# Spectral mixing plus a product-key expert layer on one core: another order of folds and transposes at the front, key products a block later, and table checks that begin one block earlier

## The chip, the cores and the metric

The kernel runs on one core of one Trainium2 chip. The metric is the device time of one launch in microseconds, the median of three runs. Lower is better.

## The reference

The output is the sum of three things for x of 2048 x 512 floats. With xn the layer norm of x over its 512 columns,

```
out = x + A(xn) + B(xn)
A:  a = xn @ Wd_re.T;  b = xn @ Wd_im.T;  y = Ws_re @ a - Ws_im @ b     (real part of a 2-D Fourier transform)
B:  q = xn @ w_q                    (32 heads, 2 x 128 each)
    s1, s2 = q1 @ k1.T, q2 @ k2.T   (64 keys each)
    the best 2 of s1 and of s2 give 4 candidates, the best 2 of them the experts and, by softmax, their weights g
    out += sum over heads and experts of g * gelu(xn . u[e]) * v[e]     (4096 experts)
```

The tables Ws and Wd come in as inputs. The kernel uses that they are Fourier tables, and it checks this on the chip.

## The kernel before

**Front (lines 230 to 560).** x stands in four groups g of 4 x 128 rows, taken in the order G = (1, 0, 2, 3). For each group VectorE and ScalarE normalize it (ln). fold(k, g) (line 358) uses the symmetry of the Fourier tables: sums (k = 0) or differences (k = 1) of quarter rows give a tile q, in six or seven VectorE instructions, whose first is fold_t (353) and whose last two write q (363 and 364). fold_row(k) (366) does the same for one single row. main(k, g) (374) multiplies q with a table on TensorE (385) and adds up over the four groups in PSUM; evict copies the result out (428). In this part there also stand the following. m_mul(0, ..) (145) makes the key products m of stage 0 (keys times a slice of w_q, so that scores come straight from x); m_scale and m_parts (line 217) scale and split them. xpose(i) (439) transposes one of the 16 tiles of x: four transposes on TensorE (445), the high 16-bit half by ScalarE (448), the low half either by a product with a negated identity idn and ScalarE (450 and 452) or by VectorE alone (454). sides() (398) makes border columns by 16 VectorE multiply-adds (394 and 396), to which GpSimd adds two rows (415 and 416).

**Scores.** Eight stages j of 16 tiles i follow: TensorE makes the scores of tile i (820), ScalarE copies them (825), VectorE takes maxima and indices (828 and 832). m_stage makes the key products of the next stage from w_q in seven steps: a load of w_q on SP (131), copies by ScalarE (155 and 160), a difference by GpSimd (163) or VectorE (157), and products on TensorE (141). The table MST (for stage 0 MST0) says behind which tile each step goes. From stage 1 on, x's halves go to a scratch tensor; in the order of SP, the first 14 of these stores stand ahead of the first loads of w_q.

**Blocks.** Then come 14 blocks b of 128 tokens. u_part(b, cg) multiplies the block with 512 experts' u (980, tile z) and ScalarE applies the gelu (983). g_mm(b, tg) builds weights g from one-hot tiles L and R that VectorE makes (1004, 1012, 1015) and TensorE multiplies (1017). w_part(b, tg) multiplies weights and gelus: VectorE (1028, tile g), ScalarE (1033) and VectorE again (1036). v_part multiplies with v (1045). z tiles take turns in a few PSUM banks; in block 1, tile 7 takes the bank of tile 4. z of blocks 0 and 1 comes first, with w_part(0, ..) and g_mm(0, ..) between; then each block's v_part is done while the next one's g and w and the z of the one after it are made. The last two token blocks are done by gathering rows: GpSimd fetches rows of u and v (1071), VectorE takes dot products with the normalized x (1087, tile px; px itself is made at 269 from xs, loaded at 1080), ScalarE and GpSimd sum up (1100, 1105).

Ahead of the first v_part, the rows of these two blocks that part A made are taken from one scratch tensor to another: a load of oy from y_d (1321), an adding transfer of x from GpSimd (1322), a store to o_d (1323), twice.

**Checks.** paced(k, mm) (1280) takes two lists of work one piece a step. One holds the fits: the largest magnitude of a piece of w_q, u or v (1215, 1216, 1222). The other holds the compares: a tile cx of a Fourier table is loaded on SP (755 and 756) and compared with its mirrored parts on VectorE (763 to 797), and ScalarE sums the magnitudes (802 and 804). VectorE's work comes two steps of its list behind the load, ScalarE's two behind that. `later` and `hold` bind a step to the product mm it follows.

The order on each engine is set by a scheduler from the order of the code, from the dependences it sees, and from added ones (pace, follow, hold); the loads wait in SP's queue one behind another.

Of the kernel before, what the change touches and what calls it, by code (L numbers as in the profile page):

```python
# [8 lines left out]
F32 = mybir.dt.float32  # L9
# [27 lines left out]
def tile_fnet_peer(ctx, tc, x, ca, cb, c5, wt, wf, wr, wq, kt, ut, vn, uv, out):  # L37
# [146 lines left out]
    def m_scale(j, pm, at=None):  # L184

        if at is not None:
            nc.vector.tensor_copy(at, one)
        mp = MP[j % 2]
        w = 1 if at is None else 3
        mx = mp.tile([P, KD + w], F32, tag="mx" if w == 1 else "mx3", name=f"mx{j}")  # L190
        m = mp.tile([P, 2, KD, 512], F16, tag="m", name=f"m{j}")
        for kd in range(KD):
            nc.scalar.activation(m[:, 0, kd, :], pm[kd], AF.Abs, scale=1.0 if at is None else at,
                                 accum_out=mx[:, kd:kd + 1])
        if w == 3:
# [6 lines left out]
        sc = mp.tile([P, 2], F32, tag="msc", name=f"msc{j}")  # L202
        nc.vector.tensor_scalar(sc[:, 0:1], q[:, 0:1], 2.0 ** 13, None, op0=ALU.mult)
        nc.vector.tensor_scalar(sc[:, 1:2], p[:, 0:1], 2.0 ** -14 / XS, None, op0=ALU.mult)
        if w == 3:
            nc.vector.tensor_scalar(wsc[:, 0:2], q[:, 1:3], 2.0 ** 12, None, op0=ALU.mult)
            nc.vector.scalar_tensor_tensor(wsc[:, 4:5], p[:, 1:2], 2.0 ** -26, p[:, 2:3], op0=ALU.mult, op1=ALU.mult)
            nc.vector.scalar_tensor_tensor(smx, q[:, 0:1], 2.0 ** 11, wsc[:, 4:5], op0=ALU.mult, op1=ALU.mult)
            nc.vector.tensor_scalar(inv1, p[:, 0:1], 2.0 ** -12 / XS, None, op0=ALU.mult)
        M[j] = m, sc[:, 1:2]  # L210
        MS[j, "s"] = sc[:, 0:1]

    def m_parts(j, pm):
        m, sc = M[j][0], MS[j, "s"]
        for kd in range(KD):
# [69 lines left out]

    FF = {}
    SM = {}

    x5 = da.tile([1, 2, 512], F32, name="x5")
    nc.scalar.dma_start(x5, x[2:4, 0, 0:1].rearrange("q p d -> p q d"))  # L290
# [2 lines left out]
    def ln(g, n):  # L293

        for q in range(4):
            if n == 0:
                st = da.tile([P, 6], F32, tag="st", name=f"st{g}_{q}", bufs=2)
            else:
                st = (FF[0, G[0]][:, 0] if n == 1 else SM[n - 1])[:, 6 * (q % 2):6 * (q % 2) + 6]
            nc.vector.bn_stats(st, xn[g][:, q])  # L300
            nc.vector.bn_aggr(mvs[:, g, q, :], st)
        var = mvs[:, g, :, 1]
        SM[n] = da.tile([P, 12], F32, tag="sm", name=f"sm{g}", bufs=2)
        sm = SM[n].rearrange("p (a q) -> p a q", a=3)
        nc.scalar.activation(sm[:, 0], var, AF.Sqrt, bias=eps)
        nc.vector.reciprocal(sm[:, 1], sm[:, 0])
        nc.vector.scalar_tensor_tensor(sm[:, 0], var, 1e-5, sm[:, 1], op0=ALU.add, op1=ALU.mult)
        nc.vector.scalar_tensor_tensor(sm[:, 2], sm[:, 0], -0.5, sm[:, 1], op0=ALU.mult, op1=ALU.mult)
        nc.vector.scalar_tensor_tensor(rstd[:, g], sm[:, 2], 1.5, sm[:, 1], op0=ALU.add, op1=ALU.mult)
        end = nc.vector.scalar_tensor_tensor(negm[:, g], mvs[:, g, :, 0], -1.0, rstd[:, g], op0=ALU.mult, op1=ALU.mult)  # L310
        if g == 0:
            nc.vector.tensor_scalar(nm0[:, 0], negm[:, 0, 2:4], not0, None, op0=ALU.mult)
            nc.vector.tensor_scalar(nm0[:, 1], rstd[:, 0, 2:4], not0, None, op0=ALU.mult)
        for q in (0, 2, 1, 3):
            t = xn[g][:, q]
            b, r = negm[:, g, q:q + 1], rstd[:, g, q:q + 1]
            if g == 0 and q > 1:
                b, r = nm0[:, 0, q - 2:q - 1], nm0[:, 1, q - 2:q - 1]
            if n == 0 and q % 2 == 0:
                norm(t, t, 4 * q + g)  # L320
            else:
                nc.scalar.activation(t, t, AF.Identity, bias=b, scale=r)
        if g == 0:
            for q in range(2):
                nc.scalar.activation(x5[:, q], x5[:, q], AF.Identity, bias=negm[0:1, 0, q + 2:q + 3],
                                     scale=rstd[0:1, 0, q + 2:q + 3])
        return end

    def fold_d(k, t, f, o, after=None):
# [19 lines left out]
    def fold_t(k, g):  # L349
# [3 lines left out]
        nc.vector.tensor_tensor(t, xn[g][:, 0:2], xn[g][:, 2:4], op=op)  # L353

    def fold(k, g, after=None):

        if after is None:
            fold_t(k, g)
# [4 lines left out]
        nc.vector.tensor_tensor(Q[k][g][:, 0, c], o[:, 0, c], o[:, 1, c], op=ALU.add)  # L363
        FF["end"] = nc.vector.tensor_tensor(Q[k][g][:, 1, c], o[:, 0, c], o[:, 1, c], op=ALU.subtract)

    def fold_row(k):
# [3 lines left out]
        if k:  # L370
            pace(i, FF["end"])
        fold_d(k, r[:, :, 0:512], r[:, :, 512:], Q[1][0][0:1, 0:1] if k else s5.unsqueeze(1))

    PP = {}
# [23 lines left out]
    def sides():  # L398


        f = FF["t"][:, 0, 0:4]
        nc.vector.tensor_copy(f[:, 0:2], Q[0][G[0]][:, :, 256])
        nc.vector.tensor_copy(f[:, 2:4], c5s[:, :, G[0]])
# [32 lines left out]
    idn = da.tile([P, P], F16, name="idn")  # L436
    nc.gpsimd.tensor_scalar(idn, ident, -1.0 / XS, None, op0=ALU.mult)

    def xpose(i, sub=False):

        p = (pb if sub and i // 4 % 2 else pc)(f"xp{i}")
        src = xn[i % 4][:, i // 4]
        for kd in range(KD):
            c = slice(kd * P, (kd + 1) * P)
            nc.tensor.matmul(p[:, c], src[:, c], ident, start=kd == 0, stop=kd == KD - 1 and not sub,
                             is_transpose=True, skip_group_check=True)
        pv = p.rearrange("p (k n) -> p k n", k=KD)
        nc.scalar.activation(xt[i][:, 0], pv, AF.Copy, scale=XS)
        if sub:
            nc.tensor.matmul(p, idn, xt[i][:, 0].rearrange("p k n -> p (k n)"), start=False, stop=True,  # L450
                             skip_group_check=True)
            nc.scalar.activation(xt[i][:, 1], pv, AF.Copy, scale=XS)
# [36 lines left out]
    wrs = uf[13][0:1, 0:129]  # L489
    nc.sync.dma_start(wrs, wr)  # L490

    for t in range(2):
        m_mul(0, t, (0, 1))
    for n, g in enumerate(G):
# [14 lines left out]
        if n == 0:  # L509
            for t in range(2):  # L510
                m_mul(0, t, (2, 3))
            for t in range(2, 4):
                m_mul(0, t, range(KD))
    evict(0)
    m_scale(0, MS[0, "p"], FF[0, G[-1]][:, 0, 0:1])
    m_parts(0, MS[0, "p"])
    nc.scalar.activation(k16[:, 0], K[0], AF.Copy, scale=sk)
    nc.vector.scalar_tensor_tensor(k16[:, 1], K[0], sk, k16[:, 0], op0=ALU.mult, op1=ALU.subtract)
    for n, g in enumerate(G):
        if n:  # L520
            fold(1, g)
        if g == 0:
            fold_row(1)
# [53 lines left out]
    def part_b(safe, stS, stP, stE, xt, u_sb, cmp_p):  # L577
# [953 lines left out]
```

## Time and profile before

| | before |
|---|---|
| median of 3 runs | 1092.44 us |
| the runs | 1088.45, 1094.63, 1092.44 us |
| profiled execution, its own time | 1090.09 us |
| its span | 1088.3 us |
| mean granted clock of TensorE | 0.995 |
| TensorE busy | 1060.8 us (97%) |
| VectorE, ScalarE, GpSimd busy | 959.6, 716.3, 608.8 us |
| DMA | 196.78 MB, mean 181 GB/s |

In a timeline, a row gives start and length in us, the engine, the line, the operation, out<-in, the count of instructions taken together, and in square brackets the idle time ahead with what ended it. SPq is the queue from which SyncE issues DMAs; its rows give the time of issue, not the landing.

### The profile page before, as it was taken

What the parts mean: (1) busy time and instruction counts of PE and PEld (TensorE: products, weight loads), DVE (VectorE), ACT (ScalarE), POOL (GpSimd) and SP (SyncE); (2) the same over time, 40 slices, a digit from 0 to 9 for tenths busy, and PEclk for the clock granted to TensorE, in tenths of its full rate; (3) what the DMA queues carried; (4) which work ended last, traced back from release to release, by engine and by line L of the source; (5) the groups of instructions that cost most, each with busy time, mean ns of one, the idle gap of its engine ahead of it and who ended that gap; (6) DMA issues with size and microseconds to landing.
All of it is one profiled execution on the core that took longest, in us unless ns stands there. A gap on an engine that the chain in (4) does not pass through costs nothing. (4 is left out here: it accounts for less than half of the span.)

```text
span 1088.3 us, 28489 instructions
## 1 busy us (share of the span) xinstructions
PE 1060.8 (97%) x11070; PEld 693.4 (64%) x11070; DVE 959.6 (88%) x2748; ACT 716.3 (66%) x1326; POOL 608.8 (56%) x553
## 2 busy tenths in 40 slices
PE   5899999999999999999999999999999999999997
PEld 4354555454544544896876958769587785867853
DVE  7978797979999999989999998999999987999871
ACT  3566657679797857545767667676666766767641
POOL 0013547588787955225655566565568766556622
PEclk9899999999999999999999999999999999999999
DMA  8257152536445341278766766775678667675611
GB/s 332 86 204 261 52 197 94 175 125 219 167 136 197 104 157 66 73 250 240 230 179 202 213 203 222 223 223 183 194 214 276 201 193 231 216 232 186 192 31 52
DMA packets 84936, 196.78 MB, mean 181 GB/s; under 512 B 10770, under 2 KB 27559, under 8 KB 84792
## 3 DMA queue, kind: packets, MB, share of 16 engines
q1 hardware_dynamic: 63898, 123.55, 33.8%
q0 software_dynamic: 20736, 71.31, 22.1%
q8 instruction: 88, 1.44, 0.5%
q14 instruction: 56, 0.46, 0.1%
q10 hardware_dynamic: 158, 0.01, 0.0%
HBM read 177.74 MB, written 17.10 MB: 179 GB/s over the span
## 5 line engine op out<-in xcount | busy, mean ns | idle before, releaser
L820 PE MATMUL s<-m,xq 128*128 128x512 f16 x1536 | 338.9, 379 | 0.0
L980 PE MATMUL z<-xb,u 128*128 128x128 f16 x5376 | 306.8, 219 | 1.2 <-DVE y L1060 1.2
L980 PEld LDWEIGHTS <-u 128*128 128x128 f16 x5376 | 301.5, 98 | 4.2 <-issue 1.3
L1045 PE MATMUL v<-v,act 128*128 128x512 f16 x1344 | 298.3, 379 | 0.0
L1105 POOL TENSOR_TENSOR ov<-ov,ga 128x512 f32<-128x512 f32 x128 | 183.8, 1436 | 186.4 <-ACT ga L1100 145.9
L820 PEld LDWEIGHTS <-xq 128*128 128x128 f16 x1536 | 148.3, 98 | 171.4 <-issue 0.2
L1045 PEld LDWEIGHTS <-act 128*128 128x128 f16 x1344 | 128.4, 98 | 146.5
L1071 POOL DMA_INDIRECT ga<-in_uv_dram,eix x128 | 159.3, 1245 | 46.0 <-POOL ov L1105 34.9
L1004 DVE TENSOR_TENSOR L<-io_lam,cmp 128x2048 f16<-128x2048 f16 x112 | 154.8, 1397 | 15.1 <-PE g L1017 15.0
L828 DVE MAX8 vals<-ss 128x8 f32<-128x64 f32 x1024 | 152.6, 216 | 17.1 <-ACT ss L825 17.0
L983 ACT ACTIVATE act<-z,scl 128x512 f32<-128x512 f32 x112 | 76.0, 682 | 103.1 <-PE z L980 102.6
L832 DVE FIND_INDEX8 idx<-vals,ss 128x8 uint16<-128x256 f32 x256 | 107.2, 419 | 0.0
L825 ACT ACTIVATE ss<-s,wsc 128x512 f32<-128x512 f32 x112 | 75.5, 681 | 43.1 <-PE s L820 33.8
L1100 ACT ACTIVATE ga<-ga,za 128x512 f32<-128x512 f32 x128 | 92.3, 722 | 9.4
L1033 ACT ACTIVATE act<-g 128x1024 f16<-128x1024 f32 x56 | 73.2, 1309 | 22.0 <-DVE g L1028 19.9
L1087 DVE SCALAR_TENSOR_TENSOR ga<-ga,px 128x512 f32<-128x512 f32 x128 | 85.8, 678 | 0.1
L1036 DVE TENSOR_TENSOR act<-g,act 128x1024 f16<-128x1024 f32 x56 | 72.9, 1303 | 14.5 <-ACT act L1033 14.3
L802 ACT ACTIVATE cx<-cx 128x896 f32<-128x896 f32 x64 | 60.6, 946 | 37.5 <-DVE cx L782 21.6
L1028 DVE SCALAR_TENSOR_TENSOR g<-act,scl,g 128x1024 f32<-128x1024 f32 x56 | 71.5, 1280 | 5.1 <-ACT act L983 3.1
L163 POOL TENSOR_TENSOR wq<-wq,wh 128x1024 f16<-128x1024 f32 x26 | 55.5, 2135 | 24.3 <-DMA cx<-in_ca_dram 15.9
L1017 PEld LDWEIGHTS <-L 128*128 128x128 f16 x1792 | 51.8, 96 | 8.4 <-DVE L L1004 1.6
L776 DVE TENSOR_TENSOR cx<-cx 128x512 f32<-128x512 f32 (+2 forms) x61 | 47.1, 804 | 11.1 <-DMA cx<-in_cb_dram 11.0
(281 smaller groups left out, 1298.8 us busy)
## 6 DMA issues: line engine op xcount, KB each, us to landing
cx<-in_cb_dram SPq DMA_DIRECT2D x50, 448.0 KB
wq<-in_wq_dram SPq DMA_DIRECT2D x32, 512.0 KB
fit<-in_wq_dram SPq DMA_DIRECT2D x28, 512.0 KB
uv<-in_ut_dram SPq DMA_DIRECT2D x16, 512.0 KB
uv<-in_vn_dram SPq DMA_DIRECT2D x16, 512.0 KB
cx<-in_cb_dram SPq DMA_DIRECT2D x28, 224.0 KB
xq<-in_x_dram SPq DMA_DIRECT2D x8, 512.0 KB
xt_d<-xq SPq DMA_DIRECT2D x16, 256.0 KB
```

Of the source, the lines that this page charges most:

```text
L820: mm = nc.tensor.matmul(ps, xt[i][:, l, kd, :], m[:, r, kd, :], start=(n == 0), stop=(n == 3 * KD - 1))
L825: done = nc.scalar.activation(s.rearrange("p g e -> p (g e)"), ps, AF.Copy, scale=inv)
L828: nc.vector.max(vals[:, i, w, :, h], s[:, g, :])
L832: nc.vector.max_index(idx[:, i, w].rearrange("p k h -> p (k h)"), vals[:, i, w, 0:2].rearrange("p k h -> p (k h)"), s[:, w * HC:g + 1, :]. ...
L980: mm = nc.tensor.matmul(p[:, cc * P:(cc + 1) * P], ug[:, l, c % 2, kd, :], xb[:, r, kd, :], start=(n == 0), stop=(n == 3 * KD - 1))
L983: GL[mm.ins.name] = nc.scalar.activation(act[:, cg * 4:cg * 4 + 4, :].rearrange("p c n -> p (c n)"), p, AF.Gelu_apprx_tanh, scale=zsc)
L1004: nc.vector.tensor_tensor(L.rearrange("p t (l two) -> p t l two", two=2), io_lam.rearrange("p (l two) -> p l two", two=2).unsqueeze(1).to_ ...
L1045: mm = nc.tensor.matmul(pv, w16[:, c, :, l], vg[:, r, c % 2, :], start=(c == 0 and k == 0), stop=(c == NC - 1 and k == 2))
L1071: nc.gpsimd.indirect_dma_start(out=t, out_offset=None, in_=uv, in_offset=bass.IndirectOffsetOnAxis(ap=eix[:, n].rearrange("p k h -> p (k h ...
L1087: nc.vector.scalar_tensor_tensor(t, t, 1.0, T["x"], op0=ALU.mult, op1=ALU.mult, accum_out=T["z", n][:, s:s + 1])
L1100: nc.scalar.activation(t, t, AF.Copy, scale=z)
L1105: T["a"] = nc.gpsimd.tensor_tensor(o, o, t, op=ALU.add)
```

## The change

Front:

- x of group 1 gets its own tile x_raw. Its transposes (xpose_a) stand between the products main(0, 1) and main(0, 2), and its low halves (xpose_b) come behind the normalization of group 3; its four tiles, like those of groups 0 and 2, all take the ScalarE way. Only the last group keeps VectorE.
- fold(1, 1) goes behind fold(0, 3), and fold_row(0) behind fold(0, 2).
- ScalarE copies the key products m from PSUM to SBUF (m_keep), so that their banks are free for the transposes. The rest of m_scale, m_parts and k16 (m_end) come behind the last fold, and sides() behind m_end.
- MST0: steps 2 to 6 of stage 0 go one tile later.

Blocks: behind each u_part(1, cg) stands a step of paced(cg % 2, mm), and the lists are spread over 102 steps instead of 98.

```diff
-        nc.vector.tensor_reduce(mx[:, KD:KD + 1], mx[:, :KD], axis=AX.X, op=ALU.max)
-        p, q = pow2(mx[:, KD:], mp, f"pw{j}", w)
...
+        def rest():
+            nc.vector.tensor_reduce(mx[:, KD:KD + 1], mx[:, :KD], axis=AX.X, op=ALU.max)
+            p, q = pow2(mx[:, KD:], mp, f"pw{j}", w)
...
+        if at is not None:
+            return rest
+        rest()
...
+    xn[1] = da.tile([P, 4, D], F32, name="x_raw")
...
     def xpose(i, sub=False):
...
+        xpose_a(i, sub)
+        xpose_b(i, sub)
...
+    def m_keep(kds, after):
+        for kd in kds:
+            pace(nc.scalar.activation(MR[kd], MS[0, "p"][kd], AF.Copy), after)
+
+    MR = [uf[2 + kd // 2][:, kd % 2 * 512:kd % 2 * 512 + 512] for kd in range(KD)]
...
         if n == 3:
-            fold(1, G[0])
-            fold_row(0)
+            fold_row(0, FF["end"])
             main_row()
+            for q in range(4):
+                xpose_b(4 * q + G[0], True, LN[3])
...
+        if n == 1:
+            m_keep((0, 2), LN[1])
+        if n in (1, 2):
+            for q in (0, 1) if n == 1 else (2, 3):
+                xpose_a(4 * q + G[0], True, LN[n + 1])
+        if n == 1:
+            m_keep((1, 3), LN[2])
         main(0, g)
...
+    fold(1, G[0])
     evict(0)
-    m_scale(0, MS[0, "p"], FF[0, G[-1]][:, 0, 0:1])
-    m_parts(0, MS[0, "p"])
-    nc.scalar.activation(k16[:, 0], K[0], AF.Copy, scale=sk)
-    nc.vector.scalar_tensor_tensor(k16[:, 1], K[0], sk, k16[:, 0], op0=ALU.mult, op1=ALU.subtract)
+    m_rest = m_scale(0, MR, FF[0, G[-1]][:, 0, 0:1])
...
     for n, g in enumerate(G):
         if n:
             fold(1, g)
...
+        if n == 3:
+            m_end(FF["end"])
         main(1, g)
-        if n:
+        if n > 1:
             for q in range(4):
-                xpose(4 * q + G[n - 1], n < 3)
+                xpose(4 * q + G[n - 1], True)
     sides()
...
-        MST0 = MST if safe else {4: 1, 5: 2, 6: 3, 7: 4, 8: 5, 9: 6}
+        MST0 = MST if safe else {4: 1, 6: 2, 7: 3, 8: 4, 9: 5, 10: 6}
...
-            for f in st[0][st[2]:-(-len(st[0]) * st[1] // (8 * (NB - 1) - 6))]:
+            for f in st[0][st[2]:-(-len(st[0]) * st[1] // (8 * (NB - 1) - 2))]:
...
         for cg in range(8):
-            u_part(1, cg)
+            mm = u_part(1, cg)
+            if not safe:
+                paced(cg % 2, mm)
```

**VectorE in the front**, from the second half of fold(0, 2) on. The number behind a name is the group: q_2_141 is q of group 2 for k = 0, q_1_144 is q of group 1 for k = 1. Before:

```order
L353 TENSOR_TENSOR ft_1_372<-xq_101 128x1024
L363 TENSOR_TENSOR q_2_141<-fo_2_360 128x257
L364 TENSOR_TENSOR q_2_141<-fo_2_360 128x257
L338 TENSOR_TENSOR ff_1_374<-ft_1_372 128x4x127
L343 TENSOR_TENSOR fo_1_375<-ft_1_372 128x2
L346 TENSOR_TENSOR fo_1_375<-ff_1_374 128x2x127
L347 TENSOR_TENSOR fo_1_375<-ff_1_374 128x2x127
L353 TENSOR_TENSOR ft_3_391<-xq_103 128x1024
```

After:

```order
L372 TENSOR_TENSOR q_2_142<-fo_2_377 128x257
L373 TENSOR_TENSOR q_2_142<-fo_2_377 128x257
L378 TENSOR_TENSOR r_0_401<-x_153 1x512
L345 TENSOR_TENSOR r_0_401<-r_0_401 1x2x127
L350 TENSOR_TENSOR s_148<-r_0_401 1x1
L360 TENSOR_TENSOR ft_3_418<-xq_103 128x1024
L353 TENSOR_TENSOR s_148<-r_0_401 1x128
L354 TENSOR_TENSOR s_148<-r_0_401 1x128
```

fold(1, 1) no longer stands between fold(0, 2) and fold(0, 3); the single row's fold does.

**SP where the blocks begin.** oy and o_d are the two last blocks' rows of part A, ov their running sum, xs the rows of x for px, cx and fit the tiles of the first compare and fit. Before:

```order
L1321 DMA oy_6821<-y_d 128x512
L1080 DMA xs_6841<-in_x_dram 128x512
L968 DMA zb_6987<-z_d 128x384
L963 DMA xb_6984<-xt_d 128x1024
L1323 DMA o_d<-oy_6821 128x512
L1321 DMA oy_6825<-y_d 128x512
L1094 DMA ov_6918<-o_d 128x512
L1323 DMA o_d<-oy_6825 128x512
L1053 DMA y_6996<-y_d 128x512
L755 DMA cx_6915<-in_ca_dram 128x128
L756 DMA cx_6915<-in_cb_dram 128x896
L1215 DMA fit_6938<-in_wq_dram 128x1024
```

After (the row of xs stands below the second o_d, behind y_7029 and a second fit):

```order
L1371 DMA oy_6860<-y_d 128x512
L1016 DMA zb_7020<-z_d 128x384
L1011 DMA xb_7017<-xt_d 128x1024
L1373 DMA o_d<-oy_6860 128x512
L1371 DMA oy_6864<-y_d 128x512
L1142 DMA ov_6960<-o_d 128x512
L803 DMA cx_6412<-in_ca_dram 128x128
L804 DMA cx_6412<-in_cb_dram 128x896
L1263 DMA fit_6502<-in_wq_dram 128x1024
L803 DMA cx_6711<-in_ca_dram 64x128
L804 DMA cx_6711<-in_cb_dram 64x896
```

The first compare's loads have moved ahead of the second o_d, but they still stand behind the first one.

**VectorE at the fourth w_part of block 0.** g_3 is its tile in PSUM, act the block's gelus, L and R the one-hot tiles for block 1, px the normalized x for the dots with gathered rows. Before:

```order
L1036 TENSOR_TENSOR act_5806<-g_2_6401,act_5806 128x32x32
L1004 TENSOR_TENSOR L_5788<-io_lam,cmp_5730 128x2048
L1028 SCALAR_TENSOR_TENSOR g_3_6541<-act_5806,scl,g_3_6541 128x32x32
L1004 TENSOR_TENSOR L_5789<-io_lam,cmp_5730 128x2048
L1036 TENSOR_TENSOR act_5806<-g_3_6541,act_5806 128x32x32
L269 TENSOR_SCALAR px_6842<-xs_6841,mvs,rstd 128x512
```

After (the next rows are the rest of the compare, act, the two L, the two steps of R, and px):

```order
L1084 TENSOR_TENSOR act_5815<-g_2_6415,act_5815 128x32x32
L811 TENSOR_TENSOR cx_6412<-cx_6412 128x256
L813 SCALAR_TENSOR_TENSOR cx_6412<-cx_6412,not_79 128x256 x2
L1076 SCALAR_TENSOR_TENSOR g_3_6568<-act_5815,scl,g_3_6568 128x32x32
L815 TENSOR_TENSOR cx_6412<-cx_6412 1x256
L830 TENSOR_TENSOR cx_6412<-cx_6412 128x2x63
```

The first compare now stands ahead of the fourth g, and the two L for block 1 have moved behind it.

More of the change, by code (lines that the diff above doesn't have):

```diff
@@ L199, in m_scale @@
                                  accum_out=mx[:, KD + 2:])
-        nc.vector.tensor_reduce(mx[:, KD:KD + 1], mx[:, :KD], axis=AX.X, op=ALU.max)
-        p, q = pow2(mx[:, KD:], mp, f"pw{j}", w)
[L202 to L211, printed above, removed]
+        def rest():
+            nc.vector.tensor_reduce(mx[:, KD:KD + 1], mx[:, :KD], axis=AX.X, op=ALU.max)
+            p, q = pow2(mx[:, KD:], mp, f"pw{j}", w)
+            sc = mp.tile([P, 2], F32, tag="msc", name=f"msc{j}")
+            nc.vector.tensor_scalar(sc[:, 0:1], q[:, 0:1], 2.0 ** 13, None, op0=ALU.mult)
+            nc.vector.tensor_scalar(sc[:, 1:2], p[:, 0:1], 2.0 ** -14 / XS, None, op0=ALU.mult)
+            if w == 3:
+                nc.vector.tensor_scalar(wsc[:, 0:2], q[:, 1:3], 2.0 ** 12, None, op0=ALU.mult)
+                nc.vector.scalar_tensor_tensor(wsc[:, 4:5], p[:, 1:2], 2.0 ** -26, p[:, 2:3], op0=ALU.mult, op1=ALU.mult)
+                nc.vector.scalar_tensor_tensor(smx, q[:, 0:1], 2.0 ** 11, wsc[:, 4:5], op0=ALU.mult, op1=ALU.mult)
+                nc.vector.tensor_scalar(inv1, p[:, 0:1], 2.0 ** -12 / XS, None, op0=ALU.mult)
+            M[j] = m, sc[:, 1:2]
+            MS[j, "s"] = sc[:, 0:1]
+        if at is not None:
+            return rest
+        rest()
     def m_parts(j, pm):
@@ L287, in tile_fnet_peer @@
     SM = {}
+    LN = {}
     x5 = da.tile([1, 2, 512], F32, name="x5")
@@ L321, in ln @@
             else:
-                nc.scalar.activation(t, t, AF.Identity, bias=b, scale=r)
+                LN[n] = nc.scalar.activation(t, t, AF.Identity, bias=b, scale=r)
         if g == 0:
             for q in range(2):
-                nc.scalar.activation(x5[:, q], x5[:, q], AF.Identity, bias=negm[0:1, 0, q + 2:q + 3],
-                                     scale=rstd[0:1, 0, q + 2:q + 3])
+                LN[n] = nc.scalar.activation(x5[:, q], x5[:, q], AF.Identity, bias=negm[0:1, 0, q + 2:q + 3],
+                                             scale=rstd[0:1, 0, q + 2:q + 3])
         return end
@@ L347, in fold_d, with fold_t @@
         nc.vector.tensor_tensor(o[:, :, P + k:2 * P], f[:, :, k:P], f[:, :, P + k:], op=po)
-    def fold_t(k, g):
+    def fold_t(k, g, after=None):
         op = ALU.subtract if k else ALU.add
         t = FF["t"] = da.tile([P, 2, 512], F32, tag="ft", name=f"ft{k}_{g}", bufs=1)
-        nc.vector.tensor_tensor(t, xn[g][:, 0:2], xn[g][:, 2:4], op=op)
+        i = nc.vector.tensor_tensor(t, xn[g][:, 0:2], xn[g][:, 2:4], op=op)
+        if after is not None:
+            pace(i, after)
     def fold(k, g, after=None):
         if after is None:
-            fold_t(k, g)
+            fold_t(k, g, FF.get("end"))
         f = da.tile([P, 2, 256], F32, tag="ff", name=f"ff{k}_{g}", bufs=2)
@@ L364, in fold, with fold_row @@
         FF["end"] = nc.vector.tensor_tensor(Q[k][g][:, 1, c], o[:, 0, c], o[:, 1, c], op=ALU.subtract)
-    def fold_row(k):
+    def fold_row(k, end):
         r = da.tile([1, 1, 768], F32, tag="r5", name=f"r5_{k}")
         i = nc.vector.tensor_tensor(r[:, 0, 0:512], x5[:, 0], x5[:, 1], op=ALU.subtract if k else ALU.add)
-        if k:
-            pace(i, FF["end"])
+        pace(i, end)
         fold_d(k, r[:, :, 0:512], r[:, :, 512:], Q[1][0][0:1, 0:1] if k else s5.unsqueeze(1))
@@ L401, in sides @@
         f = FF["t"][:, 0, 0:4]
-        nc.vector.tensor_copy(f[:, 0:2], Q[0][G[0]][:, :, 256])
-        nc.vector.tensor_copy(f[:, 2:4], c5s[:, :, G[0]])
+        pace(nc.vector.tensor_copy(f[:, 0:2], Q[0][G[0]][:, :, 256]), FF["m"])
+        pace(nc.vector.tensor_copy(f[:, 2:4], c5s[:, :, G[0]]), FF["m"])
         for n, g in enumerate(G):
@@ L437, in tile_fnet_peer, with xpose_a @@
     nc.gpsimd.tensor_scalar(idn, ident, -1.0 / XS, None, op0=ALU.mult)
+    XP = {}
     def xpose(i, sub=False):
-        p = (pb if sub and i // 4 % 2 else pc)(f"xp{i}")
+        xpose_a(i, sub)
+        xpose_b(i, sub)
+    def xpose_a(i, sub, after=None):
+        p = XP[i] = (pb if sub and i // 4 % 2 else pc)(f"xp{i}")
         src = xn[i % 4][:, i // 4]
@@ L447, in xpose, with xpose_b @@
         pv = p.rearrange("p (k n) -> p k n", k=KD)
-        nc.scalar.activation(xt[i][:, 0], pv, AF.Copy, scale=XS)
+        hi = nc.scalar.activation(xt[i][:, 0], pv, AF.Copy, scale=XS)
+        if after is not None:
+            pace(hi, after)
+    def xpose_b(i, sub, after=None):
+        p = XP.pop(i)
+        pv = p.rearrange("p (k n) -> p k n", k=KD)
         if sub:
@@ L451, in xpose @@
                              skip_group_check=True)
-            nc.scalar.activation(xt[i][:, 1], pv, AF.Copy, scale=XS)
+            lo = nc.scalar.activation(xt[i][:, 1], pv, AF.Copy, scale=XS)
+            if after is not None:
+                pace(lo, after)
             return
@@ L513, in tile_fnet_peer, with m_end @@
                 m_mul(0, t, range(KD))
+    fold(1, G[0])
     evict(0)
-    m_scale(0, MS[0, "p"], FF[0, G[-1]][:, 0, 0:1])
-    m_parts(0, MS[0, "p"])
-    nc.scalar.activation(k16[:, 0], K[0], AF.Copy, scale=sk)
-    nc.vector.scalar_tensor_tensor(k16[:, 1], K[0], sk, k16[:, 0], op0=ALU.mult, op1=ALU.subtract)
+    m_rest = m_scale(0, MR, FF[0, G[-1]][:, 0, 0:1])
+    def m_end(after):
+        made = nc.cur_bb.bb.instructions
+        first = len(made)
+        m_rest()
+        m_parts(0, MR)
+        nc.scalar.activation(k16[:, 0], K[0], AF.Copy, scale=sk)
+        FF["m"] = nc.vector.scalar_tensor_tensor(k16[:, 1], K[0], sk, k16[:, 0], op0=ALU.mult, op1=ALU.subtract)
+        for i in made[first:]:
+            if i.engine == mybir.EngineType.DVE:
+                tc.add_manual_dep(i, after.ins.name, mybir.DependencyInfo(
+                    mybir.DependencyClass.NoSync, mybir.DependencyReason.DATA), reason="pace")
     for n, g in enumerate(G):
@@ L522, in tile_fnet_peer @@
         if g == 0:
-            fold_row(1)
+            fold_row(1, FF["end"])
             nc.scalar.activation(xn[0][0:1, 2:4], x5, AF.Copy)
+        if n == 3:
+            m_end(FF["end"])
         main(1, g)
-        if n:
+        if n > 1:
             for q in range(4):
-                xpose(4 * q + G[n - 1], n < 3)
+                xpose(4 * q + G[n - 1], True)
     sides()
```

## The prediction

> **What bounds the kernel now.** I read the page first, then the waits of TensorE, then timelines of the two stretches that the diff touches.
>
> ```profile
> PE 1060.8 (97%) x11070; PEld 693.4 (64%) x11070; DVE 959.6 (88%) x2748; ACT 716.3 (66%) x1326; POOL 608.8 (56%) x553
> ```
>
> PE is busy for 97% of the span. A change here pays only where it takes away idle time of PE, and it costs wherever it makes a wait that PE sees. The waits of PE (in total, times, longest):
>
> ```profile
> PE m L145 <- DMA wq<-in_wq_dram: 9.9, 1, 9.9
> PE p L385 <- DVE q L363: 6.4, 3, 5.0
> ```
>
> The first is the start, which the diff leaves alone; the 6.4 us are the front's waits for folds. They are the two largest of the list. PE's timeline of the front, down to the first key product:
>
> ```profile
> 16.76 4.65 PE L385 MATMUL p<-c,q 128*128 128x512 f32 x8
> ...
> 29.93 6.61 PE L385 MATMUL p<-c,q 128*128 128x512 f32 x8 [5.00 <-DVE q L363]
> ...
> 43.54 10.57 PE L385 MATMUL p<-c,q 128*128 128x512 f32 x24 [0.85 <-DVE q L363]
> 54.27 1.75 PE L445 MATMUL xp<-ident,xq 128*128 128x128 f32 x10 [0.16 <-DVE m L217]
> 55.99 0.38 PE L450 MATMUL xp<-xq,idn 128*128 128x512 f16 x1
> ...
> 85.58 0.20 PE L141 MATMUL m<-sums,wq 128*128 128x64 f16 x1 [1.19 <-POOL wq L163]
> ```
>
> **The front, and what it gives.** With fold(1,1) behind fold(0,3), the folds of k=0 come sooner, so the two short waits (6.4 - 5.0 = 1.4 us) should go. Sixteen transposes (four tiles of group 1) move into the gap before and behind the product at 29.93: 16 x 0.175 = 2.8 us that PE no longer does at 54.27. Four products with idn are new, at most 4 x 0.38 = 1.5 us. PE alone would gain 1.4 + 2.8 - 1.5 = 2.7 us; that is the upper end.
>
> What decides is when the first key product has its weights, since PE waits for them already. Their chain:
>
> ```profile
> 57.91 0.88 DVE L394 TENSOR_SCALAR u<-c,ft 128x512 f32<-128x512 f32 x2
> ```
> ```profile
> 62.18 4.60 POOL L415 TENSOR_TENSOR u<-u,r 1x512 f32<-1x512 f32 x1 [10.74 <-DVE u L396]
> 66.75 0.73 POOL L416 TENSOR_TENSOR u<-u,r 1x257 f32<-1x257 f32 x1
> 83.39 2.14 POOL L163 TENSOR_TENSOR wq<-wq,wh 128x1024 f16<-128x1024 f32 x1 [15.91 <-DMA cx<-in_ca_dram]
> ```
> ```profile
> 74.90 2.08 SPq L131 DMA_DIRECT2D wq<-in_wq_dram  x4
> ```
> ```profile
> 80.50 1.15 ACT L155 ACTIVATE wh<-wq,wsc 128x1024 f16<-128x1024 f32 x1 [3.21 <-DMA wq<-in_wq_dram]
> 81.55 0.67 ACT L825 ACTIVATE ss<-s,msc 128x512 f32<-128x512 f32 x1
> ```
>
> The load at 74.90 reuses a buffer and stands behind the stores of x on SP. In the new order sides() (57.91) starts only after the last fold and m_end; walking DVE through its new rows puts it at about 63.95, 6.05 us later. POOL's step of 62.18 goes with it, to 68.2, and ends with L416 at 68.2 + 4.6 + 0.7 = 73.5. The load is issued at about 73.6, 1.3 us sooner than before, and no earlier however fast PE is. The score copy at 81.55 no longer stands between ACT's two steps on wq: 0.6 us more. So the first key product comes 1.9 us sooner. I take 1.9, with 0 and 2.7 as ends.
>
> The lower end is the clock. Its granted share (PEclk) around the gap, the column behind the busy shares:
>
> ```profile
> 28.00:29.00 1.00, 0.00 (x0) 0.00 (x0) 1.00 (x5) 1.00 (x2) 0.00 (x0) 0.99 0.06 25
> 29.00:30.00 1.00, 0.07 (x1) 0.08 (x1) 1.00 (x3) 0.97 (x2) 0.00 (x0) 0.50 0.06 25
> ```
>
> PE idles from 24.93 (29.93 - 5.00), and the clock halves at 29.0, after 4.1 us; the product then takes 6.61 instead of 4.65 us. With eight transposes (1.4 us) ahead, the new gap is 26.3 to about 29.6, 3.3 us, so by that row the clock stays up. If it falls, 2.0 us go and the front gives nothing.
>
> [...]
>
> The other edits cost nothing that the end sees. ACT's four copies of m (about the same size as its other 128x512 copies) run while PE works on main(0,·). Lower halves of group 2 go from DVE to ACT, both with room there. MST0 moves key products between score tiles that PE works through without a gap.
>
> **The compares, and what they cost.** The second part starts paced() at z of block 1. What it adds to each queue counts: loads on SP, the compare on DVE, the judging on ACT. SP before:
>
> ```profile
> 465.45 0.45 SPq L963 DMA_DIRECT2D xb<-xt_d  x1
> 482.17 0.32 SPq L1323 DMA_DIRECT2D o_d<-oy  x1
> 484.19 0.32 SPq L1321 DMA_DIRECT2D oy<-y_d  x1
> 484.56 0.42 SPq L1094 DMA_DIRECT2D ov<-o_d  x1
> 491.57 0.32 SPq L1323 DMA_DIRECT2D o_d<-oy  x1
> 495.06 0.32 SPq L1053 DMA_DIRECT2D y<-y_d  x1
> 495.43 0.81 SPq L755 DMA_DIRECT2D cx<-in_ca_dram  x1
> 496.29 0.42 SPq L756 DMA_DIRECT2D cx<-in_cb_dram  x1
> ```
> ```profile
> 476.83 1.00 POOL L1322 DMA_DIRECT2D oy<-in_x_dram  x1 [9.20 <-DMA oy<-y_d]
> ```
>
> The store of oy at 482.17 waits for POOL's adding transfer, which itself began only at 476.83. In the new order the first compare's two loads stand right behind o_d, oy and ov on SP. They can't be issued before 484.56 + 0.42 = 485.0, the second of them at 485.9. A landing takes between 2.0 us (482.17 to 484.19, where oy waits for the store's landing) and 4.1 us (496.29 to the compare at 500.42, below). The middle gives T = 489.0, the ends 488 and 490.
>
> On DVE, however, that compare now stands right behind the third act step of block 0 and ahead of its fourth g:
>
> ```profile
> 476.32 1.31 DVE L1036 TENSOR_TENSOR act<-g,act 128x1024 f16<-128x1024 f32 x1
> 477.52 1.22 DVE L1004 TENSOR_TENSOR L<-io_lam,cmp 128x2048 f16<-128x2048 f16 x1
> 478.64 1.29 DVE L1028 SCALAR_TENSOR_TENSOR g<-act,scl,g 128x1024 f32<-128x1024 f32 x1
> ...
> 482.53 0.79 DVE L269 TENSOR_SCALAR px<-xs,mvs,rstd 128x512 f32<-128x512 f32 x1
> ...
> 500.42 0.43 DVE L763 TENSOR_TENSOR cx<-cx 128x256 f32<-128x256 f32 x1
> ...
> 501.55 0.68 DVE L1087 SCALAR_TENSOR_TENSOR ga<-ga,px 128x512 f32<-128x512 f32 x1
> ...
> 502.16 0.41 DVE L767 TENSOR_TENSOR cx<-cx 1x256 f32<-1x256 f32 x1
> ...
> 503.20 0.06 DVE L797 MEMSET cx<- 128x1 f32 x1
> ```
>
> DVE is free for it at 477.5 and stands until T, 11.5 us, with g and everything behind it. ACT's copy of that g (479.97) and the gelus of z behind it stand too:
>
> ```profile
> 479.97 1.32 ACT L1033 ACTIVATE act<-g 128x1024 f16<-128x1024 f32 x1 [3.16 <-DVE g L1028]
> 481.15 1.48 ACT L983 ACTIVATE act<-z,scl 128x512 f32<-128x512 f32 x2
> ```
> ```profile
> 476.38 10.88 PE L980 MATMUL z<-xb,u 128*128 128x128 f16 x192
> 487.10 0.95 PE L1017 MATMUL g<-R,L 128*128 128x32 f16 x32
> ...
> 493.08 0.95 PE L1017 MATMUL g<-R,L 128*128 128x32 f16 x32
> ```
>
> The 192 products are four tiles of z, so the last began at 476.38 + 8.16 = 484.5; it writes the bank that the gelu of the first of the four must empty. That gelu is now done at T + 1.13 (compare, 500.42 to 501.55) + 1.33 (g, 478.64 to 479.97) + 1.18 (copy, to 481.15) + 0.74 (gelu) = T + 4.4 = 493.4. PE waits 8.9 us. Next come g of block 1, part 0, whose two L DVE makes after the compare's rest (1.1), act (1.31) and 2 x 1.22: T + 7.4 = 496.4. It ends at about 497 instead of 488.05.
>
> Part 1 comes later still. Its second L stands on DVE behind px, and px needs xs, whose load now follows y (495.06) and one more load: issue 495.9, landing by the same 2.0 to 4.1 us between 497.9 and 500, say 499. Then px 0.79, a piece of the second compare (at most 1.13), L 1.22, g 1.29, two dots of 0.68 and L 1.22: 506.0, part 1 ends near 506.5 instead of 493.08 + 0.95 = 494.0. The delay there is 12.4 us; without any wait for xs it would be 9.0, with the late landing 13.4. The halved clock behind an 8.9 us gap is hidden: PE's work up to part 1 would end by 502.4, and 2 to 3 us more still fit. After that the load queue is as before, the compares are spread a little thinner (102 steps for 98), PE works without gaps, and nothing gives the delay back; the tail is paced by PE as before.
>
> [...]
>
> **Sum.** 12.4 - 1.9 = 10.5 us. The profiled execution took 1090.09 us (span 1088.3), 2.35 under the median of the three runs, 1092.44. So 1100.6 for an execution like the profiled one, 1102.9 for the median. Ends of this case: 9.0 - 2.7 = 6.3 and 13.4 - 0, that is 1098.7 to 1105.8.
>
> **The rivals.** A: the compare's data are there in time, and only the front counts. PE's last z waits for nothing if T + 4.4 is at most 484.5, so T at most 480.1, with an issue by 477. For it: SP issues nothing between 465.9 and 482.17, and loads put ahead of the waiting store would land. Against it: the order of SP has them behind it, and the store waits for POOL's 476.83. Then 1092.44 - 1.9 = 1090.5: not slower, within what can be told from no change. 0.14.
> B: the adding transfer comes 5 us sooner, as the load of xs no longer shares the queues with oy; T, and with it the delay, shrink by 5: 1097.9. Against it, xs was issued behind oy and is a small part of what moves there. 0.08.
> C: a second stall follows, as ACT has to judge the first fit ahead of the next gelu and later compares come late again; one more landing of 4.1 us and little else: about 1107. For it, DVE has only 12% of slack over the program. 0.06.
>
> **How the numbers follow.** The summed case has 0.72. 0.5% of 1092.44 is 5.5 us, about what a measurement of this kernel can tell from no change. The range 1091 to 1108 holds most of the summed case, B and C and about half of A. Slower by over 5.5 us: nearly all of the summed case, C, part of B, 0.77. Within: most of A, part of B, the low edge of the summed case, 0.19. Faster: A with an unexpectedly large front, 0.04.
>
> **What would show it.** In the profile of the changed kernel: a wait of PE for z of about 9 us near 484 to 493, released by ACT's gelu; DVE idle for some 11 us before L811, released by the load of cx; the loads of cx on SP behind o_d; then a wait of PE for L of about 3 us near 502; in the front one wait for q of about 3.3 us at full clock and the first key product near 83.7. I am wrong if L811 waits little, or if SP issues cx before the store.

## The result, and the profile after

| | before | after |
|---|---|---|
| median | 1091.43 us (4 runs, 1088.45 to 1094.63) | 1101.73 us (4 runs, 1101.25 to 1105.32) |
| ratio, with its 95% interval | | 1.0099 (1.0076 to 1.0122) |
| profiled execution, its own time | 1090.09 us | 1105.32 us |
| mean granted clock in the profiled execution | 0.995 | 0.988 |

The changed kernel is slower by 10.3 us between the medians. Between the two profiled executions it is 15.2 us: the profiled one of after is the longest of its four, 3.6 us above the other three, whose listed clock is 0.991. So the waits read below may be longer than in the other three.

The waits of TensorE in the changed kernel come first, as in the forecast; the columns are who waited for whom, the total, how often, and the longest:

```profile
PE z L1028 <- ACT act L1031: 11.0, 1, 11.0
...
PE g L1065 <- DVE L L1052: 5.0, 3, 3.2
PE p L393 <- DVE q L372: 3.4, 1, 3.4
```

The list has a new head, z waiting for a gelu. The wait for L has grown from 1.4 to 5.0 us, and the front's wait for folds has gone from 6.4 to 3.4 us. PE's timeline where the blocks begin shows where the waits for the gelu and for L stand:

```profile
474.16 8.20 PE L1028 MATMUL z<-xb,u 128*128 128x128 f16 x144
493.40 4.42 PE L1028 MATMUL z<-xb,u 128*128 128x128 f16 x48 [11.04 <-ACT act L1031]
497.66 0.95 PE L1065 MATMUL g<-R,L 128*128 128x32 f16 x32
...
505.41 0.56 PE L1065 MATMUL g<-R,L 128*128 128x32 f16 x16 [1.61 <-DVE L L1052]
509.16 0.61 PE L1065 MATMUL g<-R,L 128*128 128x32 f16 x16 [3.18 <-DVE L L1052]
509.60 10.00 PE L1093 MATMUL v<-v,act 128*128 128x512 f16 x36
```

The second part of g of block 1 ends at 509.16 + 0.61 = 509.77 us, where before it ended at 494.03: 15.7 us later, although z began 2.2 us sooner (474.16 for 476.38). VectorE over the same stretch shows whom it waits for:

```profile
473.30 1.30 DVE L1084 TENSOR_TENSOR act<-g,act 128x1024 f16<-128x1024 f32 x1
489.07 0.43 DVE L811 TENSOR_TENSOR cx<-cx 128x256 f32<-128x256 f32 x1 [14.46 <-DMA fit<-in_wq_dram]
...
490.21 1.28 DVE L1076 SCALAR_TENSOR_TENSOR g<-act,scl,g 128x1024 f32<-128x1024 f32 x1
...
502.55 0.81 DVE L275 TENSOR_SCALAR px<-xs,mvs,rstd 128x512 f32<-128x512 f32 x1 [4.83 <-DMA xs<-in_x_dram]
```

The compare of L811 holds VectorE for 14.46 us, and only then comes g (490.21), on which ScalarE's copy and the gelus hang. The row names the load of fit, which no operation of L811 reads; the load that the compare needs is that of cx, issued just ahead of it, and in e2_paced (below) the same row names cx. SP's queue gives the cause:

```profile
480.37 0.32 SPq L1373 DMA_DIRECT2D o_d<-oy  x1
482.44 0.32 SPq L1371 DMA_DIRECT2D oy<-y_d  x1
482.81 0.42 SPq L1142 DMA_DIRECT2D ov<-o_d  x1
483.28 0.42 SPq L803 DMA_DIRECT2D cx<-in_ca_dram  x1
483.75 0.43 SPq L804 DMA_DIRECT2D cx<-in_cb_dram  x1
...
493.66 0.34 SPq L1373 DMA_DIRECT2D o_d<-oy  x1
497.32 0.33 SPq L1101 DMA_DIRECT2D y<-y_d  x1
...
498.22 0.38 SPq L1128 DMA_DIRECT2D xs<-in_x_dram  x1
```

cx is issued behind the first o_d and the second oy, and xs behind the second o_d, as the order said. The compare begins 5.3 us after its second load was issued (483.75 to 489.07), px 4.3 us after xs.

### The profile page after: what moved, and what is told of

The parts are those of the page before. It is cut to its first block, busy times and chain, and to the rows that moved or that the text cites. A ratio compares the mean times of both kernels' runs of the same rounds, so it can differ in the third digit from the quotient of the medians.

```text
span 1103.5 us, 28493 instructions
## 1 busy us (share of the span) xinstructions
PE 1065.6 (97%) x11074; PEld 696.0 (63%) x11074; DVE 959.5 (87%) x2744; ACT 719.0 (65%) x1334; POOL 607.2 (55%) x553
## 4 chain that ended last, share of the span: by engine, by line
PE 84%; DVE 8%; DMA 4%; ACT 2%; issue 1%; POOL 1%; SPq 1%; DVEq 0%; POOLq 0%
PE v L1093 25%; PE s L868 25%; PE z L1028 24%; PE g L1065 4%; PE p L393 2%; PE m L141 2%; DVE vals L876 1%; DMA oy<-y_d 1%; DVE idx L880 1%; DVE L L1052 0%; DMA x_raw<-in_x_dram 0%; DVE u L404 0%; DMA wq<-in_wq_dram 0%; DVE g L1076 0%; DMA fit<-in_wq_dram 0%
## 5 line engine op out<-in xcount | busy, mean ns | idle before, releaser
L1153 POOL TENSOR_TENSOR ov<-ov,ga 128x512 f32<-128x512 f32 x128 | 178.3, 1393 | 193.5 <-ACT ga L1148 133.7
L1119 POOL DMA_INDIRECT ga<-in_uv_dram,eix x128 | 164.1, 1282 | 57.1 <-POOL ov L1153 33.0
L1065 PE MATMUL g<-R,L 128*128 128x32 f16 x1792 | 53.8, 176 | 5.5 <-DVE L L1052 5.0
```

The costliest lines, as they stand in the source:

```text
L1065: i = nc.tensor.matmul(p[:, hf, t * NC:(t + 1) * NC], L[:, t, :], R[:, hf * 16 + t, :], start=True, stop=True)
L1119: nc.gpsimd.indirect_dma_start(out=t, out_offset=None, in_=uv, in_offset=bass.IndirectOffsetOnAxis(ap=eix[:, n].rearrange("p k h -> p (k h ...
L1153: T["a"] = nc.gpsimd.tensor_tensor(o, o, t, op=ALU.add)
```

## The experiments

The theory after the result: the whole loss is made at this place, by loads that SP issues behind a waiting store, and the front gives its gain and nothing else. The rivals: the front loses something too (the clock), or the checks cost by their mere work or by another wait later. Ratios are to the kernel before; medians in us.

| kernel | ratio (95%) | median | what of the change it holds |
|---|---|---|---|
| e1_front | 0.9972 (0.9959 to 0.9984) | 1088.28 | front alone |
| e2_paced | 1.0138 (1.0116 to 1.0160) | 1106.66 | early checks alone |
| e3_order | 1.0086 (1.0067 to 1.0105) | 1100.45 | all, cx loaded ahead of the store |
| e7_xsonly | 1.0042 (1.0023 to 1.0061) | 1097.38 | all, xs loaded early |
| e6_xs | 0.9969 (0.9957 to 0.9981) | 1087.92 | all, both |
| e5_mst | 0.9963 (0.9937 to 0.9989) | 1086.84 | front without the new MST0 |
| e8_warm | 0.9980 (0.9962 to 0.9998) | 1088.49 | front, more work for PE ahead of the gap |
| e9_all | 0.9961 (0.9946 to 0.9975) | 1087.50 | e6_xs and e8_warm |

The kernel before had a median of 1091.42 beside e1, e2, e3 and e6, and of 1092.30 beside the others.

**The two parts apart.** e1_front takes the checks of block 1 out of the changed kernel:

```diff
-            for f in st[0][st[2]:-(-len(st[0]) * st[1] // (8 * (NB - 1) - 2))]:
+            for f in st[0][st[2]:-(-len(st[0]) * st[1] // (8 * (NB - 1) - 6))]:
...
-            mm = u_part(1, cg)
-            if not safe:
-                paced(cg % 2, mm)
+            u_part(1, cg)
```

> Only the front's edits and MST0; the lists of checks start where they did before. If the whole loss comes from the checks that start a block earlier, this one keeps the front's gain alone, about 2 us: ratio to before 0.998, near 1089.3 us, with PE's first key product near 83.5 us. Rival: if the front itself gives back later what it wins at the first key product, the ratio is 1.000 or above.

e2_paced puts the same lines into the kernel before.

> Only the step of paced() at z of block 1 and the 102 steps; the front is as before. The theory (the compare waits on VectorE for a load that stands behind the store of oy on SP) gives the whole stall without the front's gain: about 12.4 us, ratio 1.011, near 1104 us, with VectorE idle over 11 us ahead of the first compare. Rival: if part of the loss came from the front, this kernel loses clearly less than the whole change does, 10 us or less.

The front alone gains 3.1 us (1091.42 - 1088.28), with an interval of 0.16% to 0.41%; what was expected, 0.998, lies in it. The checks alone lose 15.2 us (1106.66 - 1091.42), more than the 12.4 expected. The front as a whole loses nothing, and the loss is made by the checks: -3.1 and 15.2 are 12.1, for 10.3 measured, and the two agree within the intervals. The row of the first key product in e1_front:

```profile
83.57 0.20 PE L141 MATMUL m<-sums,wq 128*128 128x64 f16 x1 [0.84 <-POOL wq L163]
```

It comes 2.0 us sooner than before (85.58). In e2_paced VectorE's rows are like those of the changed kernel, the long wait for cx and then that for xs:

```profile
489.71 0.42 DVE L763 TENSOR_TENSOR cx<-cx 128x256 f32<-128x256 f32 x1 [13.69 <-DMA cx<-in_cb_dram]
...
504.83 0.81 DVE L269 TENSOR_SCALAR px<-xs,mvs,rstd 128x512 f32<-128x512 f32 x1 [6.48 <-DMA xs<-in_x_dram]
```

**The order of the loads.** e3_order leaves all work in and only makes SP issue the store of oy behind the loads of the compares:

```diff
+        LD = {}
...
-                nc.sync.dma_start(tf[e, P:], cb[ri, g, kk, a].rearrange("p b c -> p (b c)"))
+                LD["x"] = nc.sync.dma_start(tf[e, P:], cb[ri, g, kk, a].rearrange("p b c -> p (b c)"))
...
-            nc.sync.dma_start(o_d[n], o)
+            i = nc.sync.dma_start(o_d[n], o)
+            follow(i.ins, LD["x"])
```

> The whole change, but on SP the store of oy is put behind the loads of the first two compares; nothing moves on VectorE, ScalarE or PE. The theory: the loads are issued near 465 us, the compare no longer waits, PE's wait for z near 484 us goes. What stays is the wait of px for xs, whose load is still behind the second store: PE waits for L of block 1, part 1, some 8 to 9 us in place of 16 to 17, so about 4 to 6 us better than the whole change, ratio to before 1.003 to 1.007, 1095 to 1099 us. Rival (the compare's place on VectorE costs by its work and not by its wait): no better than the whole change, 1101 us.

It missed: 1.0086 is above what was expected, and by its time alone the kernel can't be told from the rival, nor from the changed kernel (1.0099). The rows decide against the rival: the compare is nearly free, and z with it, as VectorE's and PE's rows of this kernel show:

```profile
477.55 0.42 DVE L812 TENSOR_TENSOR cx<-cx 128x256 f32<-128x256 f32 x1 [3.96 <-DMA cx<-in_cb_dram]
...
497.87 0.81 DVE L275 TENSOR_SCALAR px<-xs,mvs,rstd 128x512 f32<-128x512 f32 x1 [11.65 <-DMA xs<-in_x_dram]
```

```profile
481.89 2.84 PE L1029 MATMUL z<-xb,u 128*128 128x128 f16 x48 [0.53 <-ACT act L1032]
...
500.73 0.61 PE L1066 MATMUL g<-R,L 128*128 128x32 f16 x16 [10.02 <-DVE L L1053]
504.48 0.61 PE L1066 MATMUL g<-R,L 128*128 128x32 f16 x16 [3.13 <-DVE L L1053]
504.92 9.93 PE L1094 MATMUL v<-v,act 128*128 128x512 f16 x36
```

z's wait has shrunk from 11.04 to 0.53 us, and the waits for L have grown from 1.61 + 3.18 to 10.02 + 3.13. xs still stands behind the second o_d on SP (issue at 494.47), so px waits, and the L behind px. Taking away the first wait laid the second one bare. The expectation that the first wait could be taken off by itself fell here; the new theory was that the two lie beside each other. The forecast's own times would have said so: its px at 499, and part 1 at 506.5 behind it, hang on the load of xs and not on the compare. The two profiled executions are further apart than the medians, 4.9 us (1105.32 to 1100.40).

e7_xsonly tests it from the other side: it has the order of the changed kernel, but loads xs ahead of z of block 1, into the buffer of ov. The load of ov then comes later, at 497.99 instead of 482.81.

```diff
+        XS0 = []
+        def xs_load(n):
+            b = NB + n
+            xs = (bp.tile([P, 2 * D], F32, tag="w", name=f"xs_{n}", bufs=WB)[:, :D] if n else
+                  bp.tile([P, D], F32, tag="ov", name=f"xs_{n}", bufs=1))
+            nc.sync.dma_start(xs, x[b // 4, b % 4])
+            return xs
...
-            xs = bp.tile([P, 2 * D], F32, tag="w", name=f"xs_{n}", bufs=WB)[:, :D]
+            xs = XS0.pop() if XS0 else xs_load(n)
...
-            nc.sync.dma_start(xs, x[b // 4, b % 4])
...
+        if not safe:
+            XS0.append(xs_load(0))
```

> The whole change with xs loaded early, into the buffer of ov, and the compare's loads left behind the store of oy. It gives the price of the compare's wait without that of px. By the prediction's terms: the last z of block 1 waits about 9 us, and nothing more comes on top: 9 to 10 us less the front's 3.1, ratio to before 1.005 to 1.007. If the wait of px is all that counts (the two waits lie beside each other, and the run before showed 9.4 us over before for px alone), it is 1.000 or below.

e6_xs has both edits. (The run before, of which these two expectations speak, is e3_order.)

> As the run before, and xs is loaded ahead of z of block 1 into the buffer of ov, so px needn't wait either. The theory: both waits go, PE works through z, g and v of blocks 0 and 1 without a gap, and only the front's gain is left: ratio to before 0.998, near 1089.3 us. Rival (the checks cost something at their new place whatever they wait for): 1094 us or above.

e7_xsonly came out a little under what was expected, though its interval reaches into it; the other case, 1.000 or below, is excluded. e6_xs came out as its theory said, within its interval, and its rival is excluded; two short waits stayed, though. PE's rows of e7_xsonly, then those of e6_xs:

```profile
492.66 4.08 PE L1029 MATMUL z<-xb,u 128*128 128x128 f16 x48 [11.24 <-ACT act L1032]
...
503.55 0.56 PE L1066 MATMUL g<-R,L 128*128 128x32 f16 x16 [0.44 <-DVE L L1053]
```

```profile
481.92 2.84 PE L1029 MATMUL z<-xb,u 128*128 128x128 f16 x48 [0.39 <-ACT act L1032]
...
492.78 0.56 PE L1066 MATMUL g<-R,L 128*128 128x32 f16 x16 [1.64 <-DVE L L1053]
493.19 7.93 PE L1094 MATMUL v<-v,act 128*128 128x512 f16 x36
```

Against e6_xs, which has 0.39 and 1.64 us of these waits left, the ratios give 0.0073 (8.0 us) for the compare's wait alone, 0.0117 (12.8 us) for that of xs alone, and 0.0130 (14.2 us) for both, each uncertain by some 2.5 us. 8.0 + 12.8 - 14.2 = 6.6 us are common to both, uncertain by some 4 us. With both all but gone, the whole change is worth 0.9969, as much as its front alone.

**The front's own terms.** e5_mst is e1_front with the MST0 of before.

> Only the front's edits, but MST0 as before. If the later key products matter, PE waits for weights again at the second step and part of the front's 3.1 us goes: 0.998 to 0.999 of before. If not, 0.997 as with the front.

Its interval covers that of e1_front, so in time the later key products can't be told from nothing. In its trace, PE waits once for weights of a key product, 0.6 us, and not again at the second step. e8_warm is e1_front with the transposes of the two tiles of group 1 that stand ahead of the gap done three times (they write the same values), so that the gap is shorter:

```diff
-        for kd in range(KD):
+        for kd in range(KD) if i not in (1, 5) else [*range(KD)] * 3:
```

> Only the front's edits, and the transposes of the first two tiles of group 1 are made three times over (16 more transposes on PE in the gap ahead of main(0,0)), which writes the same values. If the halved clock behind the gap costs the front 1 to 2 us and PE's time reaches the first key product, main(0,0) takes 4.7 us in place of 6.5 and the kernel is 1 to 2 us faster than with the front alone: ratio to before 0.9955 to 0.9965. If the chain of the weights decides alone, it stays at 0.997.

It missed: 0.9980 is above the expected 0.9955 to 0.9965, and its interval holds the other case, 0.997. e9_all joins it with e6_xs.

> Front, checks a block earlier with cx ahead of the store and xs early, and the repeated transposes: the best of all by the theory, 0.995 to 0.996 of before, 1086 us. Rival: the gains lie on the same chain, then it stays at 0.997.

The interval of e9_all holds both its forecast and its rival, 0.997, so it decides nothing. PE's front in e8_warm, and behind it in the changed kernel:

```profile
26.00 2.79 PE L459 MATMUL xp<-ident,x_raw 128*128 128x128 f32 x24
30.45 3.70 PE L393 MATMUL p<-c,q 128*128 128x512 f32 x8 [1.66 <-DVE q L372]
...
36.58 3.70 PE L393 MATMUL p<-c,q 128*128 128x512 f32 x8 [1.13 <-DVE q L372]
```

```profile
25.39 1.09 PE L459 MATMUL xp<-ident,x_raw 128*128 128x128 f32 x8 [0.57 <-issue]
29.87 6.71 PE L393 MATMUL p<-c,q 128*128 128x512 f32 x8 [3.38 <-DVE q L372]
...
37.72 3.60 PE L393 MATMUL p<-c,q 128*128 128x512 f32 x8
```

At full clock (granted 1.00 from 26 to 36 us in e8_warm, 0.50 from 30 to 35 us in the changed kernel) the product takes 3.70 us for 6.71, and then PE waits 1.13 us for the next q of VectorE. That q comes 6.1 us behind the one before it in both kernels (29.98 to 36.10, and 29.41 to 35.52). So the next product begins 6.13 us behind the first in e8_warm (30.45 to 36.58) and 7.85 us in the changed kernel (29.87 to 37.72): of the 3.0 us 1.7 are left, and e8_warm's time (0.9980) is not below e1_front's (0.9972). With the clock up, as in e8_warm, VectorE's folds pace this stretch.

## Why the prediction was right, and where it was not

**The mechanism: right.** Each link that was forecast is in the rows above: cx behind o_d on SP, VectorE held at L811 (14.46 us in which no step behind it on VectorE began), z waiting for the gelu at 493, then px for xs and PE for L. Moving one of the loads alone (e3, e7) took away its own wait, and moving both (e6) brought the time back, which shows them as the cause. Rival A (the compare's data are there in time) did not come; e6_xs brings it about, with xs early too: 1087.92, where A was priced at 1090.5. B (the adding transfer comes 5 us sooner) did not happen: POOL began it at 476.26 for 476.83. C was a second stall at a later compare; no such row is in the list of waits.

**The sum: right between medians, short in the profile.** It said 12.4 - 1.9 = 10.5; the medians give 10.3, but between the two profiled executions, whose rows the sum speaks of, it is 15.2. That 10.5 met 10.3 so closely is in part luck, since these steps were off.

*The front* was put at 1.9, and e1_front gives 3.1. Its two short waits went and the first key product came at 83.50, as forecast (83.7), but by another route:

```profile
75.51 1.78 SPq L131 DMA_DIRECT2D wq<-in_wq_dram  x4
...
78.85 1.15 ACT L155 ACTIVATE wh<-wq,wsc 128x1024 f16<-128x1024 f32 x1 [0.31 <-DMA wq<-in_wq_dram]
```

The loads of w_q were to be issued at 73.6, 1.3 us sooner; they were issued at 75.51, 0.6 us later than before (74.90). The walk of VectorE's rows had put sides() at 63.95, and it began at 65.72, 1.8 us later. VectorE stood for ScalarE's half of m_parts, which stands behind copies of transposes that had waited 6.32 us for PE:

```profile
61.73 0.75 DVE L222 SCALAR_TENSOR_TENSOR m<-u,msc,m 128x512 f16<-128x512 f32 x1 [3.88 <-ACT m L221]
```

GpSimd's steps went with sides(), and ended at 75.29 instead of 73.5. The loads landed faster instead: the first copy began 3.3 us after the issue, 5.6 us before. No run here settles why; ahead of them, from 72 to 74 us, the DMA share was 0.01, and 0.71 before. That ScalarE's score copy no longer stands between its two steps on w_q is as forecast.

*The clock in the front* was to stay up, and fell, at about 29.1 by its means (1.00 from 28 to 29 us, 0.57 in the next one, 0.50 from 30 on), within the gap of 3.38 us. This step failed, and so did its price: 2.0 us and no gain left. In e1_front the clock was halved too (0.50 from 26 to 35 us; its product took 6.47 us) and the front gained 3.1. The product lost 3.0 us (6.71 for 3.70), but by e8_warm a full clock would start the next one 1.7 us sooner and no more, as VectorE's q comes no sooner, and its time shows no gain.

*The wait for the compare* was put at 8.9 us on PE, and is 11.04. T, the start of the compare, was forecast at 489.0 and is 489.07, but that is luck. The front had moved everything some 2 us forward, the loads too, so they were issued at 483.3 instead of 485.0; and they took 5.3 us to be of use, not 2.0 to 4.1. PE came to its wait 2.2 us sooner for the same T.

*The load of xs* was the largest miss. It was put at 495.9, and px at 499; they are 498.22 and 502.55. The forecast had moved xs past y and had left y itself where it was. But y and xs stand behind the second o_d, and that store waits for POOL's second adding transfer. POOL's row of before, then that of after:

```profile
487.59 0.87 POOL L1322 DMA_DIRECT2D oy<-in_x_dram  x1 [9.75 <-DMA oy<-y_d]
```

```profile
485.73 0.87 POOL L1372 DMA_DIRECT2D oy<-in_x_dram  x1 [8.47 <-DMA oy<-y_d]
```

From this row to the issue of the second o_d it is 491.57 - 487.59 = 4.0 us before and 493.66 - 485.73 = 7.9 us after. The transfer starts 1.9 us sooner and its store comes 2.1 us later. The six loads of compares and one of fits that SP now issues from 483.28 to 486.62 run at the same time; the DMA share of a window is the last column but one, first before, then after:

```profile
484.00:493.00 9.00, 9.00 (x115) 6.25 (x113) 5.95 (x9) 4.16 (x8) 1.96 (x2) 1.00 0.54 143
```

```profile
484.00:493.00 9.00, 0.00 (x0) 0.00 (x0) 3.58 (x13) 1.48 (x2) 0.87 (x1) 0.64 0.91 250
```

That these loads slow the transfer is read from rows that go together; no run varies them alone. The other kernels agree with it. Where the compare loads stand right behind oy, the second adding transfer takes 7.2 (e2_paced) and 8.3 us (e7_xsonly); where they don't, 4.4 (e1_front), 4.6 (e3_order) and 4.1 (e6_xs). In the last two the last compare loads are issued beside the first adding transfer (at 474.50 and 475.12, the transfer at 473.15 and 474.90), and there it takes 8.9 and 8.3 us for 5.3 before.

*"The halved clock is hidden"* held for the gap that it spoke of: the 48 products of z took 4.42 us, begun at the halved clock (0.50 from 488 to 496 us, 1.00 from 497 on), for 2.84 in e3_order (1.00 there), with PE waiting for L behind them anyway. It did not hold for the gap after that one:

```profile
506.00:508.00 2.00, 0.00 (x0) 0.75 0.59 176
508.00:510.00 2.00, 0.84 (x18) 0.50 0.00 0
510.00:512.00 2.00, 2.00 (x6) 0.50 0.04 8
```

The clock, the third number from the right, falls a second time within the second wait for L (505.98 to 509.16), and the 36 products of v that follow take 10.00 us (9.93 in e3_order, at 0.50 from 497 to 508 us) for 7.93 in e6_xs (at 1.00). These 2.1 us lie on the path and were not in the sum.

*"Nothing gives the delay back"* was wrong by about as much. Before, PE still waited twice behind this place, for L and for a y of VectorE:

```profile
597.08 0.56 PE L1017 MATMUL g<-R,L 128*128 128x32 f16 x16 [1.06 <-DVE L L1004]
792.34 10.88 PE L980 MATMUL z<-xb,u 128*128 128x128 f16 x192 [1.25 <-DVE y L1060]
```

Neither wait is in the changed kernel, nor in e6_xs; e1_front still has both (1.08 and 1.69). The 2.3 us that they cost before come back here. That the earlier and thinner checks are what freed the two places is argued, not shown. In e6_xs, waits of 0.39 and 1.64 us at the start of the blocks take back most of that, which agrees with its ending level with e1_front.

So the profiled executions add up as 15.7 us at the second part of g, 2.1 us of clock, less 2.3 us: 15.5, for 15.2 measured. What made the other three executions 3.6 us shorter stays open: their listed clock is higher (0.991 for 0.988), but no trace of them shows where.

## What to carry to other kernels

On SP's queue here a moved load came no sooner than the waiting store ahead of it: cx at 483.28, behind the first o_d at 480.37, and xs at 498.22, behind the second at 493.66. So follow each moved load back to the store that waits, and that store back to what it waits for, and reckon with that very transfer taking longer while the new loads are under way (7.9 us for 4.0 here). When two waits come from the same queue, price each with the other one gone, because they can lie beside each other, as here: between the medians, curing the first alone gave 1.3 us back here, which can't be told from nothing, and curing both 13.8 (1101.73 to 1100.45 and to 1087.92). The earlier start of the checks cost 15.2 us with its loads behind the waiting store (e2_paced), and nothing that can be told from the front alone once they and xs had a place ahead of it (e6_xs, 1087.92 for 1088.28).

## What the runs showed that was not expected

The same gap of PE in the front, 3.38 us long, did not meet the clock in the same way in every execution. In e6_xs the clock fell when PE had already been busy again for over a microsecond; in the changed kernel, while PE still idled:

```profile
30.00:31.00 1.00, 0.99 (x3) 1.00 0.06 25
31.00:32.00 1.00, 1.00 (x3) 0.62 0.06 25
```

```profile
29.00:30.00 1.00, 0.13 (x1) 0.13 (x1) 1.00 (x3) 1.00 (x3) 0.00 (x0) 0.57 0.06 25
```

(PE begins at 30.01 and 29.87.) In e8_warm the gap of 1.66 us left the clock at 1.00. But in e1_front its mean is 0.79 from 24 to 26 us and 0.50 from 26 on; a single fall that gives this lies near 25.2, within a gap of 0.83 us that ends at 25.30, and the clock stayed down through the longer gap behind it:

```profile
25.30 1.94 PE L459 MATMUL xp<-ident,x_raw 128*128 128x128 f32 x8 [0.83 <-issue]
29.79 6.47 PE L393 MATMUL p<-c,q 128*128 128x512 f32 x8 [2.54 <-DVE q L372]
```

So in these rows the length of the gap alone does not decide, and that the clock fell after 4.1 us before was no ground for expecting it to stay up over 3.3 us. In e6_xs the drop came 1.2 us into the next work and 4.6 us after the last transposes (near 31.24 by the mean of 0.62 from 31 to 32 us, for 30.01 and 26.63).
